# The last 64 rows of an attention tile: one full-array product and a pair of half-array products in place of two full-array products

## The chip, the cores and the metric

The kernel runs on one core of one Trainium2 chip. The metric is the time on the device in microseconds (us); the median of several executions stands for a kernel. The engines are TensorE (PE: products and transposes, with its weight loads shown as PEld), VectorE (DVE), ScalarE (ACT), GpSimd (POOL) and the queue of SyncE (SP), which issues all DMAs here.

## The reference

A linear-attention block whose output is gated by a feed-forward block, on 2048 tokens of width 576 in float32:

```python
xn = layernorm(x)                                   # 2048 x 576
q, k, v = split(xn @ wqkv)                          # 32 heads of 18
phi = lambda t: where(t > 0, t + 1, exp(t)) + 1e-6
kv = einsum("bhsd,bhse->bhde", phi(k), v)           # state of a head
num = einsum("bhqd,bhde->bhqe", phi(q), kv)
den = einsum("bhqd,bhd->bhq", phi(q), sum_s(phi(k))) + 1e-6
s = (num / den) @ wo
g = silu(gelu(xn @ w1 + b1) @ w2 + b2)              # width 4608 in between
out = x + s * g
```

## The kernel before

**Split operands.** TensorE works on a rounded float32 type. So an operand `a` is kept as a high part `h` (a ScalarE cast) and a low part `l = a - h` (a VectorE subtraction), and a product of `a` and `w` is the sum `h*wh + l*wh + h*wl`. The part `l*wl` is small and is left out nearly everywhere.

**Attention tiles.** Once the sums over all tokens are known, the state of the heads and `wo` are folded into one matrix `kw` of 576 x 576 (`fold_wo`). What is left for a tile of 128 tokens is: divide `phi(q)` by its denominators, transpose it, and multiply it by `kw`. Depth 576 is four blocks of 128 rows and a rest of 64 (rows 512 to 575). `pad` copies columns 512 to 575 of the tile once more behind its end, and the fifth block of `kw` holds its 64 rows twice, so that block 4 has 128 rows as well: rows 0 to 63 and rows 64 to 127 hold the same values.

There are 16 such tiles. Ten of them (`TO`) are done one after the other in the stage that I call the early one, lines 1327 to 1629: `transpose_p(j)` makes the five transposes into a PSUM tile `ptp`, casts all five blocks to `th` on ScalarE, and subtracts on VectorE: into `tl` for blocks 0 to 3, and for block 4 into `th` itself, rows 64 to 127 only. Block 4 of `th` is then high above and low below. `attend_mm` issues the products: per block and pair of parts two of them, for output columns 0 to 287 and 288 to 575, each into a bank of its own of the PSUM tile `ps_s`. Blocks 0 to 3 need three pairs of parts. Block 4 needs two: [h; l] by [wh; wh] and [h; l] by [wl; wl]. So a tile has (3 x 4 + 2) x 2 = 28 products. `attend(j)` casts the sums out and stores them; the first tiles are begun early by `attend_hi`, with eight of the 14 pairs of products.

The other six tiles (`LATER_TILES`) run one by one in the second half of the feed-forward stage, as class `Attention`; its methods are spread over that stage's steps by the table `A_AT`. Here `tha` and `tla` are the operands, `pta` the transposes and `psa` the sums, and `attend_mm` is the same. The weight parts lie in `Attention.kw`; `split_folded(k)` makes them once from the stored `kw`.

**The weight's block 4.** In the early stage the fold leaves block 4 in two PSUM tiles `ps_kw`; line 1209 casts them to the high part, and `last_kw_lo` subtracts the low part into `kw_l`, two subtractions of 288 columns.

**Order.** Nothing is reordered: every engine runs its instructions as the program issues them (`in_order`), and waits where an operand or a buffer is not ready. PSUM tiles of two banks (`bank2`: `ptp`, `ps_s`, `pta`, `psa`, and those of the feed-forward stage) take turns on three places; who takes a place waits for the last reader of what was there. In the early stage tile 7's sums follow `ptp7`, `ps_s6` and `ptp8`, and so take the place of `ptp7`.

Of the kernel before, what the change touches and what calls it, by code (L numbers as in the profile page):

```python
# [8 lines left out]
F32 = mybir.dt.float32  # L9
F32R = mybir.dt.float32r  # L10
# [5 lines left out]
P = 128  # L16
S = 2048
D = 576
HD = 288
# [5 lines left out]
KT = 5  # L25
# [22 lines left out]
def linear_attention_gated_ffn(ctx, tc, x, xT, wqkv, wo, w1, w1e, b1, w2, b2, out):  # L48
    nc = tc.nc
    SUB, MUL, ADD = ALU.subtract, ALU.mult, ALU.add  # L50
# [1173 lines left out]
    def last_kw_lo():  # L1224
        for _, hs, ps in last_kw:
            h, l = (w[4][:, hs] for w in kw_ops)
            nc.vector.tensor_tensor(l, ps, h.bitcast(F32), op=SUB)

    def last_kw_copy():
        for dst, _, ps in last_kw:  # L1230
# [76 lines left out]
    def transpose_only(j):  # L1307
        pb = p_bufs[j % len(p_bufs)]
        ptps[j] = pt = bank2(f"ptp{j}").rearrange("p a b -> p (a b)")
        for k in range(KT):  # L1310
            nc.tensor.transpose(pt[:, k * P : (k + 1) * P], pb[:, k * P : (k + 1) * P], ident)
# [16 lines left out]
    thp = ph2.enter_context(tc.tile_pool(name="thp", bufs=3, side="right", reuse_waits="tile"))  # L1328
    pT = {}

    def transpose_p(j):
        if j not in ptps:
            transpose_only(j)
        pt = ptps.pop(j)
        th = thp.tile([P, KT, P], F32R, tag="th", name=f"th{j}")
        tl = thp.tile([P, KT - 1, P], F32R, tag="tl", name=f"tl{j}")
        p3 = pt[:, : KT * P].rearrange("p (k c) -> p k c", k=KT)
        nc.scalar.copy(th, p3)
        nc.vector.tensor_tensor(tl, p3[:, :4, :], th[:, :4, :].bitcast(F32), op=SUB)
        nc.vector.tensor_tensor(th[64:, 4, :], p3[64:, 4, :], th[64:, 4, :].bitcast(F32), op=SUB)  # L1340
        pT[j] = (th, tl)

    transpose_p(0)
    kw_lo(1, dve)
    kw_hi(2), kw_hi(3)
    transpose_p(1)
    phi_q_hi(TO[4])
    kw_lo(2, dve), kw_lo(3, pool)
    store_kw(3)
    last_kw_lo()  # L1350
    phi_q_max(TO[4])
    pad(2)
# [7 lines left out]
    w1p = ctx.enter_context(tc.tile_pool(name="w1p", bufs=2, reuse_waits="tile"))  # L1360
    w2rp = ctx.enter_context(tc.tile_pool(name="w2rp", bufs=1, reuse_waits="tile"))
    def attend_mm(ps, th, tl, w, part=slice(None)):
        seq = [(st, v, k) for st, v in ((th, 0), (tl, 0), (th, 1)) for k in range(4)]
        seq += [(th, 0, 4), (th, 1, 4)]
        for i, (st, v, k) in list(enumerate(seq))[part]:
            for h in range(2):
                nc.tensor.matmul(  # L1367
                    ps[:, h, :HD], st[:, k, :], w[v][k][:, h * HD : (h + 1) * HD],
                    start=(i == 0), stop=(i == len(seq) - 1),
                )  # L1370

# [2 lines left out]
    def attend_hi(j):  # L1374
        ps = begun[j] = bank2(f"ps_s{j}")
        attend_mm(ps, *pT[j], kw_ops, slice(0, 8))

    def attend(j):
        ps = begun.pop(j) if j in begun else None
        if ps is None:  # L1380
            ps = bank2(f"ps_s{j}")
            attend_mm(ps, *pT.pop(j), kw_ops)
        else:
            attend_mm(ps, *pT.pop(j), kw_ops, slice(8, None))
        s_sb = stage(D, f"s{j}")
        nc.scalar.copy(as2(s_sb), ps[:, :, :HD])
        nc.sync.dma_start(s_dram[TO[j]], s_sb)
# [201 lines left out]
    attend_hi(0), attend_hi(1)  # L1589
    by_sums(4)  # L1590
    transpose_p(2)
    denominators(3), p_mult(3)
    last_kw_copy()
# [431 lines left out]
    att = None  # L2025
# [7 lines left out]
    class Attention:  # L2033
# [15 lines left out]
        def split_folded(self, k):  # L2049
            h, l = (w[k] for w in Attention.kw)  # L2050
            src = l.bitcast(F32)
            nc.scalar.copy(h, src)
            nc.vector.tensor_tensor(l, src, h.bitcast(F32), op=SUB)

        def load_sums(self):
# [47 lines left out]

        def operands(self):
            th = att.tile([P, KT, P], F32R, tag="e", name=f"tha{self.t}")
            tl = att.tile([P, KT - 1, P], F32R, tag="tl", name=f"tla{self.t}")
            p3 = self.pt[:, : KT * P].rearrange("p (k c) -> p k c", k=KT)
            nc.scalar.copy(th, p3)
            nc.vector.tensor_tensor(tl, p3[:, :4, :], th[:, :4, :].bitcast(F32), op=SUB)
            nc.vector.tensor_tensor(  # L2110
                th[64:, 4, :], p3[64:, 4, :], th[64:, 4, :].bitcast(F32), op=SUB
            )
            self.ops = th, tl

        def product(self):
            attend_mm(self.ps, *self.ops, Attention.kw)
# [36 lines left out]
    seq = ExitStack()  # L2153
    seq.enter_context(in_order(nc.vector.engine, nc.scalar.engine, nc.gpsimd.engine, nc.tensor.engine))
    n_chunks = 2 * NC
    for step in range(n_chunks):
# [3 lines left out]
        h = HOps(c)  # L2160
# [12 lines left out]
        if half == 0:  # L2173
# [7 lines left out]
            if (c, 5) not in w2_dram:  # L2181
                w = w2t[step]
# [17 lines left out]
        elif not plain:  # L2200
# [8 lines left out]
            else:  # L2209
                make(W2, w2t, step + 1)  # L2210

                w = w2t[step + 1]
# [118 lines left out]
```

## Time and profile before

| | |
|---|---|
| median of 3 runs | 1082.27 us (1081.86 to 1082.9) |
| profiled execution | 1081.32 us, span 1079.6 us |
| TensorE busy | 1071.5 us of the span, granted clock 0.999 |
| VectorE, ScalarE, GpSimd busy | 825.2, 528.3, 533.5 us |
| products of the attention tiles (L1367) | 448, each 128 x 128 weights by 288 columns |

The span runs from the first to the last instruction in the profile; the execution's time has 1.7 us around it. A row of the timeline gives the start in us from the span's start, the length of the merged record, engine, line, operation, output and inputs, active rows and columns of the array for TensorE, shapes, and a count. In brackets stands how long the engine idled before it and what ended that. The records of TensorE's products overlap, since the next starts while earlier ones are still in the array; the distance between starts is what a product costs in a stream. A row of the view of one line or tile gives minimum, median and maximum duration in ns, first and last start, and the shapes; a row of the view by groups gives the count, busy us and mean ns of one.

### The profile page before, as it was taken

Reading aid. Unit: us, or ns where it says so; the run is one execution under the profiler, and the core shown is the slowest. Engines: PE = TensorE matmul, PEld = TensorE weight load, DVE = VectorE, ACT = ScalarE, POOL = GpSimd, SP = SyncE. Lnnn points to the kernel's source line nnn. Section 1 sums busy time; section 2 is a strip of 40 time slices with the busy share of each in tenths; the row PEclk is TensorE's granted clock in tenths of the full one; section 3 lists DMA queues with packets and bytes.
Section 4 is the critical chain, followed back from the end, with each engine's and each line's share of the span. In section 5 each row is a group of like instructions: output and inputs, shape, how many; then the busy total and the mean of one; then the engine's idle time right before and its main releaser. Section 6 shows DMA issues by size and latency. Waiting matters only on the chain.

```text
span 1079.6 us, 17941 instructions
## 1 busy us (share of the span) xinstructions
PE 1071.5 (99%) x6500; PEld 990.7 (92%) x6500; DVE 825.2 (76%) x1202; ACT 528.3 (49%) x880; POOL 533.5 (49%) x552
## 2 busy tenths in 40 slices
PE   9999999999999999999999999999999999999998
PEld 7999999998998989989899898998989899998988
DVE  7997765768998898988989886485847566574856
ACT  7656657736455454554545545253443434242442
POOL 3133131658577695775957744143443525242340
PEclk9999999999999999999999999999999999999999
DMA  6678635798658577585675797796756657666653
GB/s 241 197 287 232 230 115 183 272 385 313 246 216 312 187 261 267 209 313 182 250 286 205 275 393 277 271 311 209 232 195 226 219 182 245 202 225 229 213 154 135
DMA packets 91122, 258.63 MB, mean 240 GB/s; under 512 B 12183, under 2 KB 25495, under 8 KB 88730
## 3 DMA queue, kind: packets, MB, share of 16 engines
q1 hardware_dynamic: 91034, 257.49, 68.3%
q8 instruction: 51, 0.84, 0.3%
q14 instruction: 37, 0.30, 0.1%
HBM read 155.45 MB, written 101.10 MB: 238 GB/s over the span
## 4 chain that ended last, share of the span: by engine, by line
PE 95%; DVE 2%; POOL 1%; issue 1%; DMA 1%; ACT 0%; SPq 0%; POOLq 0%; DVEq 0%
PE pm L1837 35%; PE a L1671 11%; PE zy L1671 11%; PE e L1671 11%; PE b L1671 5%; PE xaall L392 4%; PE x L392 4%; PE pd L1958 2%; PE x1all L392 2%; PE psa L1367 2%; PE ps_kva L482 1%; PE xakv L392 1%; PE x0all L392 1%; PE ps_s L1367 1%; PE x1kv L392 1%; POOL bs L1158 1%
## 5 line engine op out<-in xcount | busy, mean ns | idle before, releaser
L1774 POOL TENSOR_TENSOR g<-g 128x256 f32<-128x256 f32 x204 | 185.6, 938 | 56.9 <-DVE h_l L1419 49.9
L1843 DVE TENSOR_TENSOR macc<-pm,macc 128x576 f32<-128x576 f32 x218 | 163.8, 751 | 42.2 <-PE pm L1837 41.4
L1416 ACT CAST h_h<-g 128x512 fp32r<-128x512 f32 x204 | 122.7, 621 | 117.4 <-PE pm L1837 116.3
L1419 DVE TENSOR_TENSOR h_l<-g,h_h 128x512 fp32r<-128x512 f32 x204 | 165.1, 816 | 2.0 <-ACT h_h L1416 2.0
L1671 PE MATMUL a<-X,wa 128*128 128x512 f32 x432 | 110.2, 390 | 0.0
L1671 PEld LDWEIGHTS a<-X,wa 128*128 128x128 f32 x432 | 79.8, 188 | 15.4
L1688 ACT COPY mid<-a 128x512 f32<-128x512 f32 x36 | 21.1, 585 | 112.0 <-PE a L1671 112.0
L1774 POOL TENSOR_TENSOR mid<-g 128x256 f32<-128x256 f32 x68 | 52.0, 785 | 43.6 <-ACT g L1679 42.5
L1691 DVE TENSOR_TENSOR mid<-b,mid 128x512 f32<-128x512 f32 x36 | 24.8, 689 | 62.0 <-PE b L1671 62.0
L1467 POOL TENSOR_TENSOR w1raw<-w1raw 128x256 f32<-128x256 f32 x18 | 13.3, 739 | 91.3 <-ACT h_h L1416 47.7
L1679 ACT ACTIVATE g<-b,b1c 128x512 f32<-128x512 f32 x36 | 24.8, 689 | 66.9 <-DVE b L1697 66.8
L1671 PE MATMUL e<-X,wc 128*128 128x512 f32 x216 | 55.4, 392 | 0.0
L1671 PE MATMUL zy<-X,wd 128*128 128x512 f32 x216 | 54.9, 389 | 0.0
L1671 PE MATMUL zy<-X,wc 128*128 128x512 f32 x216 | 54.8, 389 | 0.0
L1671 PE MATMUL e<-X,wd 128*128 128x512 f32 x216 | 54.8, 389 | 0.0
L276 POOL TENSOR_TENSOR R<-R,bc 128x640 f32<-128x640 f32 x9 | 16.3, 1826 | 70.2 <-DMA R<-xT 38.8
L1671 PEld LDWEIGHTS zy<-X,wd 128*128 128x128 f32 x216 | 40.5, 188 | 8.6
L1671 PEld LDWEIGHTS e<-X,wd 128*128 128x128 f32 x216 | 40.5, 188 | 8.4
L1671 PEld LDWEIGHTS zy<-X,wc 128*128 128x128 f32 x216 | 40.5, 188 | 8.4
L1671 PEld LDWEIGHTS e<-X,wc 128*128 128x128 f32 x216 | 40.1, 188 | 8.1
L1679 ACT ACTIVATE g<-e,b1c 128x512 f32<-128x512 f32 x36 | 24.8, 689 | 45.3 <-DVE e L1704 45.3
L2090 POOL TENSOR_TENSOR qa<-qa,dena 128x576 f32<-128x576 f32 x6 | 7.0, 1168 | 62.4 <-issue 56.6
(1032 smaller groups left out, 3216.0 us busy)
## 6 DMA issues: line engine op xcount, KB each, us to landing
we<-we_dram SPq DMA_DIRECT2D x72, 224.0 KB, 5.5
w2raw<-w SPq DMA_DIRECT2D x10, 1152.0 KB
x_dram<-X SPq DMA_DIRECT2D x6, 1792.0 KB, 10.7
w1raw<-w SPq DMA_DIRECT2D x18, 512.0 KB, 4.5
op_a<-wa SPq DMA_DIRECT2D x18, 512.0 KB, 4.6
op_c<-wc SPq DMA_DIRECT2D x18, 512.0 KB, 2.6
op_d<-wd SPq DMA_DIRECT2D x18, 512.0 KB, 5.2
wc<-op_c SPq DMA_DIRECT2D x18, 512.0 KB, 5.4
```

The lines of the kernel that those rows point to most:

```text
L392: nc.tensor.matmul(dst, st, w, start=start, stop=stop, skip_group_check=True)
L1367: nc.tensor.matmul(ps[:, h, :HD], st[:, k, :], w[v][k][:, h * HD : (h + 1) * HD], start=(i == 0), stop=(i == len(seq) - 1),)
L1416: nc.scalar.copy(pair[0], src)
L1419: eng.tensor_tensor(pair[1], src, pair[0].bitcast(F32), op=SUB)
L1671: nc.tensor.matmul(ps, st, mv, start=first and n == 0, stop=n == len(seq) - 1, skip_group_check=True,)
L1679: nc.scalar.activation(g, ps, AF.Gelu_apprx_tanh, bias=b1c[:, f : f + 1])
L1688: nc.scalar.copy(m1_sb, A)
L1691: tt(u1_sb, B, m1_sb, op=ADD)
L1774: nc.gpsimd.tensor_tensor(dst[:, cs], a[:, cs], b[:, cs], op=op)
L1837: nc.tensor.matmul(ps[:, q, :HD], hs[p][st][:, cs], m[:, p, :], start=(n == 0 and i not in CHAIN), stop=(n == 5), skip_group_check=True,)
L1843: nc.vector.tensor_tensor(dst, src, dst, op=ADD)
L1958: nc.tensor.matmul(ps, st[:, cs], w_all.rearrange("p n d -> p (n d)")[:, w], start=(i == 0), stop=(i == len(seq) - 1),)
```

## The change

Block 4 is formed otherwise. The weight's second operand becomes a stack: rows 0 to 63 hold the high part once more, rows 64 to 127 the low part. The tile's high part stays as it is in all 128 rows, and its low part goes to a place of its own (`t4`, and a fifth block of `tla`). Then one pair of products over all 128 rows, `th` block 4 by [wh; wl], gives `h*wh + h*wl`. The part `l*wh` comes from two products of 64 rows: output columns 0 to 287 from rows 0 to 63 in the array's upper half, columns 288 to 575 from rows 64 to 127 in its lower half. What falls away is `l*wl` of these 64 rows. There are still 28 products in a tile.

```diff
     def last_kw_lo():
         for _, hs, ps in last_kw:
             h, l = (w[4][:, hs] for w in kw_ops)
-            nc.vector.tensor_tensor(l, ps, h.bitcast(F32), op=SUB)
+            nc.scalar.copy(l[:64], ps[:64])
+            nc.vector.tensor_tensor(l[64:], ps[64:], h[64:].bitcast(F32), op=SUB)
...
         tl = thp.tile([P, KT - 1, P], F32R, tag="tl", name=f"tl{j}")
+        t4 = thp.tile([P, P], F32R, tag="t4", bufs=2, name=f"t4{j}")
...
         nc.vector.tensor_tensor(tl, p3[:, :4, :], th[:, :4, :].bitcast(F32), op=SUB)
-        nc.vector.tensor_tensor(th[64:, 4, :], p3[64:, 4, :], th[64:, 4, :].bitcast(F32), op=SUB)
-        pT[j] = (th, tl)
+        nc.vector.tensor_tensor(t4, p3[:, 4, :], th[:, 4, :].bitcast(F32), op=SUB)
+        pT[j] = (th, [tl[:, k, :] for k in range(4)] + [t4])
...
     def attend_mm(ps, th, tl, w, part=slice(None)):
+        th = [th[:, k, :] for k in range(KT)]
         seq = [(st, v, k) for st, v in ((th, 0), (tl, 0), (th, 1)) for k in range(4)]
-        seq += [(th, 0, 4), (th, 1, 4)]
+        seq += [(th, 1, 4), (tl, 0, 4)]
         for i, (st, v, k) in list(enumerate(seq))[part]:
             for h in range(2):
+                rows = slice(64 * h, 64 * h + 64) if i == len(seq) - 1 else slice(0, P)
                 nc.tensor.matmul(
-                    ps[:, h, :HD], st[:, k, :], w[v][k][:, h * HD : (h + 1) * HD],
+                    ps[:, h, :HD], st[k][rows], w[v][k][rows, h * HD : (h + 1) * HD],
                     start=(i == 0), stop=(i == len(seq) - 1),
                 )
...
             nc.scalar.copy(h, src)
+            if k == KT - 1:
+                nc.scalar.copy(l[:64], src[:64])
+                h, l, src = h[64:], l[64:], src[64:]
             nc.vector.tensor_tensor(l, src, h.bitcast(F32), op=SUB)
...
-            tl = att.tile([P, KT - 1, P], F32R, tag="tl", name=f"tla{self.t}")
+            tl = att.tile([P, KT, P], F32R, tag="tl", name=f"tla{self.t}")
             p3 = self.pt[:, : KT * P].rearrange("p (k c) -> p k c", k=KT)
             nc.scalar.copy(th, p3)
-            nc.vector.tensor_tensor(tl, p3[:, :4, :], th[:, :4, :].bitcast(F32), op=SUB)
-            nc.vector.tensor_tensor(
-                th[64:, 4, :], p3[64:, 4, :], th[64:, 4, :].bitcast(F32), op=SUB
-            )
-            self.ops = th, tl
+            nc.vector.tensor_tensor(tl, p3, th.bitcast(F32), op=SUB)
+            self.ops = th, [tl[:, k, :] for k in range(KT)]
```

TensorE's order at the end of tile 3 of the early stage, before (`kw_l` and `kw_h` are the weight's parts, `th` the tile's high part):

```order
L1367 MATMUL ps_s_2420<-kw_l_2063,th_2362 128x288 x6
L1367 MATMUL ps_s_2420<-kw_l_2064,th_2362 128x288 x2
L1367 MATMUL ps_s_2420<-kw_h_2062,th_2362 128x288 x2
L1367 MATMUL ps_s_2420<-kw_l_2064,th_2362 128x288 x2
L1311 MATMUL ptp_2452<-ident,pbuf 128x128 x5
```

And with the change, where `t` is the new tile `t4`:

```order
L1371 MATMUL ps_s_2427<-kw_h_2062,tl_2368 128x288 x2
L1371 MATMUL ps_s_2427<-kw_l_2063,th_2367 128x288 x6
L1371 MATMUL ps_s_2427<-kw_l_2064,th_2367 128x288 x4
L1371 MATMUL ps_s_2427<-kw_h_2062,t_2369 128x288 x2
L1312 MATMUL ptp_2459<-ident,pbuf 128x128 x5
```

The two products of block 4 by the high weight's 128 rows are gone, those by the second operand have moved up, and the pair of 64 rows (the shape printed is that of the output) now ends the tile, ahead of the next transposes.

ScalarE's order where the weight's block 4 is finished, with the change; before, the row on `eq` is followed by `pbuf` at once:

```order
L434 ACTIVATE eq_2193<-eq_2193,tiny 128x576
L1227 CAST kw_l_2064<-ps_kw_2140 64x288
L1227 CAST kw_l_2064<-ps_kw_2145 64x288
L1180 COPY pbuf<-pbuf 128x64
L1340 CAST th_2266<-ptp_2260 128x640
L1232 COPY kw_1996<-ps_kw_2140 128x288
```

Two casts of 64 rows now stand ahead of the pad of tile 2 (`pbuf`), which the fifth transpose of that tile reads.

## The prediction

> **What bounds the kernel now.** I read the page's totals first, then the chain that ended last.
>
> ```profile
> span 1079.6 us, 17941 instructions
> PE 1071.5 (99%) x6500; PEld 990.7 (92%) x6500; DVE 825.2 (76%) x1202; ACT 528.3 (49%) x880; POOL 533.5 (49%) x552
> PE 95%; DVE 2%; POOL 1%; issue 1%; DMA 1%; ACT 0%; SPq 0%; POOLq 0%; DVEq 0%
> ```
>
> TensorE is busy for 99% of the span and is 95% of the chain. So a nanosecond more or less on TensorE counts fully, except where TensorE waits anyway. Next I read the products of line 1367, with their shapes kept apart, and one tile in order of time.
>
> ```profile
> L1367 PE MATMUL psa<-kw,tha x120: 290/294/302, 743.9 to 993.0; 128*128 128x288 f32 x120
> ...
> L1367 PE MATMUL ps_s<-kw_h,th x100: 288/295/401, 197.7 to 240.4; 128*128 128x288 f32 x100
> ...
> L1367 PE MATMUL ps_s<-kw_l,th x100: 292/295/377, 202.8 to 240.7; 128*128 128x288 f32 x100
> ...
> L1367 PE MATMUL ps_s<-kw_h,tl x80: 292/294/302, 199.2 to 239.1; 128*128 128x288 f32 x80
> ...
> L1367 PE MATMUL psa<-kw,tla x48: 292/294/302, 745.0 to 991.4; 128*128 128x288 f32 x48
> ```
>
> ```profile
> 743.95 1.22 PE L1367 MATMUL psa<-kw,tha 128*128 128x288 f32 x8
> 745.00 1.23 PE L1367 MATMUL psa<-kw,tla 128*128 128x288 f32 x8
> 746.07 1.75 PE L1367 MATMUL psa<-kw,tha 128*128 128x288 f32 x12
> 747.66 1.54 PE L1671 MATMUL a<-X,wa 128*128 128x512 f32 x6
> ```
>
> The rows hold 448 products: 28 in each of 16 tiles, ten between 197 and 241 us and six from 744 us on. The tile's 28 starts fill 743.95 to 747.66, so they are 0.133 us apart. Each record is 0.295 us long, so two earlier products are still in the array when one starts. That is what a switch of the array's layout could have to wait for: 0.295 - 0.133 = 0.162 us.
>
> Where does TensorE wait in these stretches? Only the early one has waits that can swallow something.
>
> ```profile
> 222.91 0.42 PE L1367 MATMUL ps_s<-kw_l,th 128*128 128x288 f32 x2
> 223.48 0.77 PE L1311 MATMUL ptp<-ident,vb 128*128 128x128 f32 x5
> ...
> 227.80 0.71 PE L1311 MATMUL ptp<-ident,pbuf 128*128 128x128 f32 x5
> 229.03 1.29 PE L1367 MATMUL ps_s<-kw_h,th 128*128 128x288 f32 x8 [0.53 <-DVE th L1340]
> ```
>
> ```profile
> L1311 PE MATMUL ptp<-ident,vb 128*128 128x128 f32 x30 | 4.3, 274 | 0.1
> ```
>
> ```profile
> 227.89 0.69 DVE L1339 TENSOR_TENSOR tl<-ptp,th 128x512 fp32r<-128x512 f32 x1
> 228.59 0.29 DVE L1340 TENSOR_TENSOR th<-ptp,th 64x128 fp32r<-64x128 f32 x1
> ```
>
> Five transposes span 0.71 us and one record is 0.274 long, so their starts are (0.71 - 0.274) / 4 = 0.109 us apart. So tile 7 could have started at 227.80 + 5 x 0.109 = 228.35 and started at 229.03: 0.69 us of waiting. At 223.48 it is 0.30 us (222.91 + 2 x 0.133 = 223.18). Together 1.0 us by which tiles 0 to 6 can be later at no cost, and which swallows what they gain. Is the wait at 229.03 removed? Its releaser is the subtraction that the change takes out of `th`. But the product waits there for PSUM: three bank pairs are used in turn, and tile 7's sums take the pair of its own transposes, whose last reader is that subtraction. The new one, into `t4`, reads the same pair at the same place. The wait stays.
>
> **VectorE.** Line 1340 becomes a subtraction over 128 rows instead of 64.
>
> ```profile
> L545 DVE SCALAR_TENSOR_TENSOR wa_rest0ef<-wa_rest0gm,sgn,wa_rest0ef 64x512 f32<-64x512 f32 x1 | 0.8, 752 | 0.0
> ...
> L543 DVE SCALAR_TENSOR_TENSOR wa_rest0ef<-wa_rest0ef,sgn 128x512 f32<-128x512 f32 x1 | 0.7, 671 | 0.0
> ```
>
> Sixty-four rows are no cheaper than 128 for the same columns, so ten times 0.29 us stay 0.29, and so do the two halved ones of line 1227. In the six late tiles two subtractions become one of 640 columns. From 0.69 us for 512 columns and 0.29 for 128, a column costs 1.03 ns, and the one takes 0.82 instead of 0.98 us: 0.16 us less on VectorE, six times. It buys nothing.
>
> ```profile
> 742.41 0.69 DVE L2109 TENSOR_TENSOR tla<-pta,tha 128x512 fp32r<-128x512 f32 x1 [2.93 <-ACT tha L2108]
> 743.13 0.29 DVE L2110 TENSOR_TENSOR tha<-pta,tha 64x128 fp32r<-64x128 f32 x1
> ```
>
> It had ended at 743.42, and TensorE came to the tile in its own order at 743.95.
>
> **ScalarE.** Added are two casts of 64x288 ahead of `pad(2)`, and one of 64x576 behind the splits of the folded weight.
>
> ```profile
> 201.37 0.23 ACT L1180 COPY pbuf<-pbuf 128x64 f32<-128x64 f32 x1
> 203.11 0.69 ACT L1338 CAST th<-ptp 128x640 fp32r<-128x640 f32 x1 [1.51 <-PE ptp L1311]
> 203.70 0.71 ACT L1231 COPY kw<-ps_kw 128x288 f32<-128x288 f32 x2
> ```
>
> ```profile
> 727.58 2.39 ACT L2052 CAST kw<-kw 128x576 fp32r<-128x576 f32 x4
> 734.02 0.59 ACT L1688 COPY mid<-a 128x512 f32<-128x512 f32 x1 [4.05 <-PE a L1671]
> ```
>
> By the 0.71 us of two copies of that length, `pad(2)` ends at 202.31 instead of 201.60.
>
> ```profile
> 202.37 0.71 PE L1311 MATMUL ptp<-ident,pbuf 128*128 128x128 f32 x5
> ```
>
> Only the fifth transpose reads the pad, at 202.37 + 4 x 0.109 = 202.81. Half a microsecond is left, and behind it ScalarE idles 1.51 us. Without that cover the 0.71 us would go on TensorE once. The late cast (some 0.6 us, a quarter of 2.39) has 4.05 idle us behind it. ScalarE: nothing.
>
> **TensorE.** Each tile keeps 28 products. The last two shrink from 128 rows to 64, one in each half of the array and each into its own bank. So there are two unknowns: whether they run at once, and what going to 64 rows and back costs. No product of 64 rows stands in the trace. The nearest rows are six products that use 8 of the array's columns.
>
> ```profile
> 192.52 0.30 PE L392 MATMUL x1q<-wT1h,X 128*128 128x288 f32 x1
> 192.65 0.30 PE L1200 MATMUL ps_kw<-wT4h,wT1h 72*8 72x288 f32 x1
> ...
> 193.31 0.29 PE L1200 MATMUL ps_kw<-wT4h,wT1l 72*8 72x288 f32 x1
> 193.44 0.29 PE L392 MATMUL xaq<-wT4h,X 128*128 128x288 f32 x1
> ```
>
> Going in takes 0.13 us and coming back 0.13 us: no price. But there only the outputs narrow, and sums still run down all rows. In the new pair the sums of the two halves must leave the array apart, while the full products ahead, two of them still inside, add both. That is why I do not carry the free switch over. The lower end for a switch is 0; for the upper end the array empties first.
>
> In the upper case, counted from the start of the last full product: it leaves at 0.295, and the pair starts then, not at 0.133. The full product behind starts another 0.295 later, at 0.590, where three steps of 0.133 made 0.400. That is 0.191 us more a tile if the pair runs at once and all weights are loaded meanwhile. If the loads wait for the switch too, 0.109 comes in at each end (starts of transposes are no closer, at 128 columns to load and to stream): 0.409. If the pair runs one after the other as well, 0.133 more: 0.542. No row is nearer to either of the first two, so I take their middle, 0.300.
>
> The Trainium skill, page "TensorEngine Tiling (Array Packing)", section "Key Properties", says that a change of the tiling mode drains TensorE. By it the sum is the upper case; the trace shows no such drain for the columns (0.13 us in, 0.13 out) and nothing for the rows.
>
> Sum: 16 x 0.300 = 4.8 us, less the 1.0 us that the waits at 223 and 229 swallow: 3.8 us. The profiled execution took 1081.32 us (span 1079.6 and 1.7 around it), so 1085.1 by it; the median of the three runs, 1082.27, lies 0.95 above, so I predict **1086.1 us**. The forecast's own range goes from 16 x 0.191 - 1.0 = 2.1 us (1084.4) to 16 x 0.542 - 1.0 = 7.7 us (1090.0).
>
> **Rivals.** First: the switch is free, as for the columns, and the pair overlaps. If the two start together, a tile saves 0.133 us. If the second waits until its weights are in, its load begins with the first product and takes 0.109, and a tile saves 0.02. What tiles 0 to 6 save is lost in the wait at 229.03, so nine tiles count: 0.2 to 1.2 us, 1081.1 to 1082.1 us, middle 1081.6. For it speaks the free switch at 192.65, against it that the rows' sums must part. The Trainium skill, page "TensorE: Matmul & The Clock Gate", section "The mechanism", has products in different row groups start about 4 ns apart. By that it is the far end, 1081.1; no row here shows it.
>
> Second, the change does not do what it says: free switch, but the halves run in turn. Then 28 steps of 0.133 remain and the time stays 1082.3.
>
> Third, faster: the halves run at once and the saving of the early tiles is kept too, because the VectorE and POOL work that ends in the wait at 229.03 moves up with TensorE. That is 16 x 0.133 = 2.1 us, and with the six late tiles' 0.16 us on VectorE, if it shortens a wait, up to 3.1: 1079.2 to 1080.1. Against it: the work behind 229.03 is named VectorE, not TensorE.
>
> **How the numbers follow.** Forecast 0.50, first rival 0.32, second 0.10, third 0.08. A difference of 0.2%, 2.2 us, is about what a measurement of this kernel can tell from no change. Faster by that is the third rival: 0.08. The first two lie within: 0.42. Slower is the forecast, whose low end just reaches the bound: 0.50. The range takes in the first rival and all but the dearest of the forecast (0.542 a tile): 1081.0 to 1089.0.
>
> **What would show it.** In the changed profile: in a late tile, 26 products at 0.133 steps, then a gap of 0.16 us or more ahead of the first 64-row product and another ahead of the next full one. Two free steps of 0.13 there would sink the forecast. The starts of the two 64-row records tell whether they run at once: some ns apart, 0.11, or 0.133. The wait at 229.03 should still end with a VectorE subtraction, and the transposes near 202.4 should show no new wait on ScalarE.

## The result, and the profile after

| | before | changed |
|---|---|---|
| median of 13 runs | 1081.44 us (1080.75 to 1082.90) | 1084.43 us (1083.73 to 1086.99) |
| ratio, 95% interval | | 1.0030 [1.0022, 1.0037] |
| span of the profiled execution | 1079.6 us | 1082.2 us |
| TensorE busy | 1071.5 us | 1075.1 us |
| VectorE busy, instructions | 825.2 us, 1202 | 817.4 us, 1196 |

The change makes the kernel 3.0 us slower, 0.30%; 3.8 us had been forecast. The two profiled executions, read below, differ by 2.6 us. The totals and the chain by engine, from the page of the changed kernel:

```profile
span 1082.2 us, 17941 instructions
PE 1075.1 (99%) x6500; PEld 990.1 (91%) x6500; DVE 817.4 (76%) x1196; ACT 529.7 (49%) x883; POOL 535.0 (49%) x552
PE 97%; POOL 1%; DMA 1%; ACT 0%; issue 0%; DVE 0%; SPq 0%; ACTq 0%; DVEq 0%
```

TensorE still bounds the kernel. Its share of the chain went from 95% to 97%, and VectorE's from 2% to 0: VectorE no longer ends a wait that counts.

What a tile now costs is read in the last late tile. First the starts of TensorE's products in the changed kernel (start, length of the merged record, count at the end of the row), then the weight loads of the same place,

```profile
993.95 1.50 PE L1371 MATMUL psa<-kw,tha 128*128 128x288 f32 x10
995.37 0.40 PE L1371 MATMUL psa<-kw,tla 64*128 64x288 f32 x2
995.70 1.65 PE L1675 MATMUL a<-X,wa 128*128 128x512 f32 x6
997.19 0.39 PE L1675 MATMUL a<-RX,we 128*128 128x512 f32 x1
```

```profile
994.75 0.45 PEld L1371 LDWEIGHTS psa<-kw,tha 128*128 128x128 f32 x3
995.37 0.19 PEld L1371 LDWEIGHTS psa<-kw,tla 64*128 64x128 f32 x2 [0.17 <-issue]
995.70 0.53 PEld L1675 LDWEIGHTS a<-X,wa 128*128 128x128 f32 x3
```

and, from the view of line 1371, the durations of the 64-row products of the early stage (minimum, median, maximum in ns):

```profile
L1371 PE MATMUL ps_s<-kw_h,t x20: 392/393/397, 204.4 to 241.6; 64*128 64x288 f32 x20
```

Four things stand in these rows.

- **The pair runs at once.** Two records of about 0.393 us make one merged record of 0.40 us, so the two starts lie within some ns; the single records of the trace have them 3 to 4 ns apart.
- **Going in waits.** The tenth full product starts at 993.95 + 9 x 0.133 = 995.15, and the pair 0.22 us later, where 0.133 was the step. That is 0.09 us.
- **The weights wait too.** In a stream a load, 0.19 us long, begins with the product before its own and is mostly hidden under it. Here the loads idle for 0.17 us and start at 995.37, at the same time as the pair's products: nothing is loaded ahead across the switch. So the records of the pair are 0.39 us long instead of 0.295; by this reading some 0.10 us of each is its own weight load. The switch is not the only place of this: behind the wait at 223.48 us in the kernel before, the first transpose starts with its own load, and five of them fill 0.77 us there instead of 0.71.
- **Coming out is the same again.** The next full product starts 0.33 us after the pair: 0.10 of load, 0.133 of streaming, 0.09 of emptying. Its own load begins with it and is not hidden either: its six products take 1.49 us to the next row, where before it was 1.38 (747.66 to 749.04).

Measured are the distances between starts. That the 0.09 us is the array running empty is a reading: the pair starts 0.07 us before the record of the product ahead ends, and no row shows the array itself.

Before, the first late tile and the six products behind it ended with this start:

```profile
749.04 0.39 PE L1671 MATMUL a<-RX,we 128*128 128x512 f32 x1
```

From the tile's start at 743.95 that is 5.09 us. The first late tile of the changed kernel shows the two ends:

```profile
744.80 1.22 PE L1371 MATMUL psa<-kw,tha 128*128 128x288 f32 x8
...
748.35 0.40 PE L1371 MATMUL psa<-kw,tla 64*128 64x288 f32 x2
748.68 1.65 PE L1675 MATMUL a<-X,wa 128*128 128x512 f32 x6
750.17 0.40 PE L1675 MATMUL a<-RX,we 128*128 128x512 f32 x1
```

744.80 to 750.17 is 5.37 us: 0.28 us more, of which the step-by-step sum (two switches of 0.09 + 0.11, less one step of 0.133 that the overlap saves) explains 0.27.

In the early stage the wait that a VectorE subtraction ended is gone. TensorE comes later than VectorE is done:

```profile
228.68 0.40 PE L1371 MATMUL ps_s<-kw_h,t 64*128 64x288 f32 x2
229.01 0.76 PE L1312 MATMUL ptp<-ident,pbuf 128*128 128x128 f32 x5
229.53 1.30 PE L1371 MATMUL ps_s<-kw_h,th 128*128 128x288 f32 x8
```

```profile
228.59 0.28 DVE L1342 TENSOR_TENSOR t<-ptp,th 128x128 fp32r<-128x128 f32 x1
```

Tile 7 starts at 229.53 with no wait; its PSUM place had been read out at 228.87. That is 0.50 us later than before, and 0.11 of it is the stage's own later start (its first transposes stand at 195.41 us, before at 195.30). The seven tiles ahead had lost about 1.6 us (0.26 for each of the first two, behind which products follow, 0.21 for the five with transposes behind them). So the old waits swallowed 1.1 to 1.2 us: the 0.99 us of waiting itself and, behind each wait, a load that was not hidden. The 0.21 is read here too: five transposes take 0.52 us to the next product, 0.05 more than the 0.47 of the kernel before, where coming out costs a full product 0.11:

```profile
232.82 0.71 PE L1311 MATMUL ptp<-ident,vb 128*128 128x128 f32 x5
233.29 1.31 PE L1367 MATMUL ps_s<-kw_h,th 128*128 128x288 f32 x8
```

The first transposes of the stage and the first product of the feed-forward stage, before and after:

```profile
195.30 0.71 PE L1311 MATMUL ptp<-ident,vb 128*128 128x128 f32 x5
...
240.82 1.55 PE L1671 MATMUL a<-X,wa 128*128 128x512 f32 x6
```

```profile
195.41 0.71 PE L1312 MATMUL ptp<-ident,vb 128*128 128x128 f32 x5
...
241.92 0.96 PE L1675 MATMUL a<-X,wa 128*128 128x512 f32 x3
```

The stage grows from 45.52 to 46.51 us, by 1.0. The rest of the span, with the six late tiles in it, grows from 838.8 us (1079.6 - 240.82) to 840.3 (1082.2 - 241.92), by 1.5.

### The profile page after: what moved, and what is told of

Read it like the earlier page. It is cut to its first block, busy times and chain, and to the rows that moved or that the text cites. A ratio compares the mean times of both kernels' runs of the same rounds, so it can differ in the third digit from the quotient of the medians.

```text
span 1082.2 us, 17941 instructions
## 1 busy us (share of the span) xinstructions
PE 1075.1 (99%) x6500; PEld 990.1 (91%) x6500; DVE 817.4 (76%) x1196; ACT 529.7 (49%) x883; POOL 535.0 (49%) x552
## 4 chain that ended last, share of the span: by engine, by line
PE 97%; POOL 1%; DMA 1%; ACT 0%; issue 0%; DVE 0%; SPq 0%; ACTq 0%; DVEq 0%
PE pm L1841 35%; PE a L1675 11%; PE zy L1675 11%; PE e L1675 11%; PE b L1675 5%; PE xaall L392 4%; PE x L392 4%; PE ps_s L1371 3%; PE pd L1962 2%; PE x1all L392 2%; PE psa L1371 2%; PE ps_kva L482 1%; PE xakv L392 1%; PE x0all L392 1%; PE x1kv L392 1%; PE ptp L1312 0%
```

## The experiments

The theory after the result: **a row switch costs twice.** Each change between the full layout and the 64-row layout empties the array (0.09 us over a step) and then leaves one weight load unhidden (0.10 to 0.11 us). Two switches a tile are 0.40 us, the overlap gives 0.133 back. The rivals: the added casts and subtractions are to blame (A); 64-row products are slow in themselves (B); the pair does not really overlap (C); the early waits swallow nothing (D); the price grows with the product ahead (E). All times over before are against runs of the kernel before on the same chip, 1081.03 us in the first four experiments and 1081.41 in the other three.

### The same edits, but 96 rows

```diff
-                rows = slice(64 * h, 64 * h + 64) if i == len(seq) - 1 else slice(0, P)
+                rows = slice(0, 96) if i == len(seq) - 1 else slice(0, P)
```

> As the change, but the two last products take rows 0 to 95 instead of 64 rows each, so they stay in the array's full layout (32 of the 64 low rows by the high weight are counted twice in the output). All edits on ScalarE and VectorE stay. Theory (the price is two switches of the array's layout a tile, each emptying the array, about 0.09 us, and then loading weights unhidden, about 0.11 us): no switch, 28 steps of 0.133 us, time as before within 0.5 us, 1081.4. Rival A (the added casts and subtractions delay the tiles): 3 us slower as the change, 1084.4.

Measured: 1081.66 us, 0.6 over before by the medians and 0.3 by the ratio, 1.0003 [0.9994, 1.0012]; the interval goes from 0.6 us faster to 1.3 us slower. The end of the last late tile:

```profile
993.02 0.69 PE L1371 MATMUL psa<-kw,tha 128*128 128x288 f32 x4
993.55 0.43 PE L1371 MATMUL psa<-kw,tla 96*128 96x288 f32 x2
993.82 1.09 PE L1675 MATMUL a<-X,wa 128*128 128x512 f32 x4
```

Two products of 96 rows take 0.27 us, two steps of 0.133, and what follows comes at once. Everything else of the change is in this kernel, so the casts and subtractions cost nothing that can be measured, and rival A with its 3 us falls. The early stage also answers a point of the prediction:

```profile
228.63 0.71 PE L1312 MATMUL ptp<-ident,pbuf 128*128 128x128 f32 x5
229.66 0.63 PE L1371 MATMUL ps_s<-kw_h,th 128*128 128x288 f32 x3 [0.31 <-DVE t L1342]
```

Without the switches the wait ahead of tile 7 is there again, and it ends with the subtraction into `t4`. Taking the subtraction out of `th` did not take the wait away, since it is one for the PSUM place.

### Both products in the same half

```diff
-                rows = slice(64 * h, 64 * h + 64) if i == len(seq) - 1 else slice(0, P)
+                rows = slice(0, 64) if i == len(seq) - 1 else slice(0, P)
```

> As the change, but both 64-row products use rows 0 to 63, the same half of the array. Theory: the switches stay, the overlap goes; the second starts 0.133 us after the first instead of 0.004, 16 x 0.13 = 2.1 us over the change, 1086.5, 5.1 over before. Rival B (a product of 64 rows is slow in itself, 0.324 us, with no price for the layout): the second takes another 0.324, 5.2 us over the change, 1089.6. Rival C (the records of the overlapping pair deceive, and it runs in turn anyway): as the change, 1084.4.

Measured: 1085.82 us, 4.8 over before, ratio 1.0040 [1.0027, 1.0053].

```profile
996.94 0.56 PE L1371 MATMUL psa<-kw,tha 128*128 128x288 f32 x3
997.43 0.53 PE L1371 MATMUL psa<-kw,tla 64*128 64x288 f32 x2
997.89 1.19 PE L1675 MATMUL a<-X,wa 128*128 128x512 f32 x4
```

The next full product now comes 0.46 us after the first of the two, not 0.33: without overlap the second costs one more step of 0.13. So the overlap in the change is real (C falls by this step; the two times alone are too close), and a second 64-row product costs no second 0.32 (B falls). The step is the one that was forecast, and the 4.8 us agree with the 5.1 forecast over before (the interval goes from 2.9 to 5.7 us). The time lies 0.7 us under the stated 1086.5; 0.4 of that is the kernel before, which took 1081.03 us in these runs and 1081.44 in those that the statement started from.

The same rows also tell the load from the switch. The second of the two follows inside the layout, and yet it starts 0.23 to 0.24 us after the first (0.53 less a record of 0.295), a step and 0.10 us: the first one's unhidden load.

### The pair twice

```diff
-        seq += [(th, 1, 4), (tl, 0, 4)]
+        seq += [(th, 1, 4), (tl, 0, 4), (tl, 0, 4)]
...
-                rows = slice(64 * h, 64 * h + 64) if i == len(seq) - 1 else slice(0, P)
+                rows = slice(64 * h, 64 * h + 64) if i >= len(seq) - 2 else slice(0, P)
```

> As the change, but the pair of 64-row products is issued twice at a tile's end (the low part by the high weight is counted twice in the output). Theory: a further pair inside the 64-row layout costs one step, 0.133 us, 16 x 0.133 = 2.1 us over the change, 1086.5. Rival B (64-row products slow in themselves): 0.324 us a pair, 5.2 us over the change, 1089.6.

Measured: 1086.34 us, 5.3 over before where 5.1 was forecast, ratio 1.0048 [1.0035, 1.0060].

```profile
997.59 0.54 PE L1371 MATMUL psa<-kw,tla 64*128 64x288 f32 x4
998.05 0.97 PE L1675 MATMUL a<-X,wa 128*128 128x512 f32 x3
```

Four 64-row products, two pairs, take 0.46 us to the next full product where one pair takes 0.33. A further pair inside the layout costs 0.13 us. So the price lies at the border of the layout and not in the products.

### Two more switches

```diff
+        steps = [(i, s, h) for i, s in enumerate(seq) for h in range(2)]
+        steps.sort(key=lambda s: (min(s[0], len(seq) - 2), s[2] if s[0] > len(seq) - 3 else 0))
```

The products are issued in the order of `steps`: full, 64 rows above, full, 64 rows below.

> As the change, but the order at a tile's end is full product, 64 rows upper half, full product, 64 rows lower half: four switches a tile instead of two, and no overlap. The same 28 products. Theory: 4 x 0.20 = 0.80 us a tile over before, 16 x 0.80 = 12.8 less the 1.0 us that the waits at 223 and 229 us swallow: 11.8 over before, 1093.2. Rival B (each 64-row product 0.324 instead of 0.133, no price for switching): 0.38 a tile, 6.1 less 1.0, 5.1 over before, 1086.5.

Measured: 1091.99 us, 11.0 over before, ratio 1.0098 [1.0085, 1.0112].

```profile
1002.01 0.69 PE L1375 MATMUL psa<-kw,tha 128*128 128x288 f32 x4
1002.63 0.40 PE L1375 MATMUL psa<-kw,tla 64*128 64x288 f32 x1
1002.95 0.40 PE L1375 MATMUL psa<-kw,tha 128*128 128x288 f32 x1
1003.28 0.39 PE L1375 MATMUL psa<-kw,tla 64*128 64x288 f32 x1
1003.60 1.43 PE L1679 MATMUL a<-X,wa 128*128 128x512 f32 x5
```

Between two switches each step is 0.32 to 0.33 us, whether a full product or a 64-row one stands there: 0.19 over a step, the 0.09 of emptying and the 0.10 of loading. The full product in the middle is just as slow as its 64-row neighbours, which no theory of slow 64-row products allows. The time was expected 0.8 us higher, inside the interval (9.2 to 12.1 us over before). The trace accounts for most of it: a tile with transposes behind it takes 0.71 us more than before (two of them 9.96 us from transposes to transposes, 222.28 to 232.24, where one took 4.27, 214.64 to 218.91) and not 0.80, which is 0.5 us over six tiles, and the waits swallow 1.1 to 1.2 us instead of 1.0.

### Early tiles alone, late tiles alone

In the first kernel the late tiles, in the second the early ones, keep operands, weight parts and products as before; for this `attend_mm` stands in the kernel twice. The core of the second one's edit:

```diff
         def product(self):
-            attend_mm(self.ps, *self.ops, Attention.kw)
+            attend_mm_pair(self.ps, *self.ops, Attention.kw)
```

> The change in the ten early tiles alone; the six late ones as before. Theory: from the changed profile a tile costs 0.26 us more where products follow and 0.21 where transposes follow: 4 x 0.26 + 6 x 0.21 = 2.3 us, less 1.0 us that TensorE waited there before: 1.3 over before, 1082.7. Rival D (the early waits move along with TensorE and swallow nothing): 2.3 over, 1083.7.

> The change in the six late tiles alone; the ten early ones as before. Theory: 6 x 0.264 = 1.6 us over before, 1083.0. Rival D (the early stage pays in full, so less is left here: 3.0 - 2.3): 0.7 over, 1082.1.

Measured: early alone 1082.64 us, 1.2 over before, ratio 1.0011 [1.0003, 1.0020]; late alone 1083.58 us, 2.2 over, ratio 1.0020 [1.0011, 1.0029]. The early value is near the theory's 1.3. Its interval, 0.3 to 2.2 us, just leaves rival D's 2.3 out; the late value is above the theory's 1.6, with an interval of 1.2 to 3.1 us that holds it and leaves rival D's 0.7 out. The two add up to 3.4 us with intervals that take in the 3.0 of the whole change.

The traces separate the two better than the times, since the stretch ahead of the early stage ends at another moment in each execution. The rows that begin and end that stage, with the early tiles changed alone and with the late ones alone:

```profile
195.69 0.71 PE L1312 MATMUL ptp<-ident,vb 128*128 128x128 f32 x5
...
242.23 1.19 PE L1685 MATMUL a<-X,wa 128*128 128x512 f32 x4
```

```profile
196.62 0.71 PE L1311 MATMUL ptp<-ident,vb 128*128 128x128 f32 x5
...
242.18 1.31 PE L1683 MATMUL a<-X,wa 128*128 128x512 f32 x5
```

| | early stage | rest of the span |
|---|---|---|
| before | 45.52 us | 838.8 us |
| early tiles alone (span 1081.1 us) | 46.54 us | 838.9 us |
| late tiles alone (span 1082.5 us) | 45.56 us | 840.3 us |
| whole change | 46.51 us | 840.3 us |
| 96 rows (span 1080.3 us) | 45.31 us | 838.9 us |

The early tiles cost 1.0 us in their stage, the late ones 1.5 in the rest, and neither stretch changes by more than 0.1 us when the other's tiles are changed. The 2.3 us that rival D needs in the early stage are not there. With 96 rows (196.11 to 241.42) neither stretch is longer than before by more than 0.1, which speaks once more against rival A. Of these 2.3 us of added steps the last load, 0.1, falls behind the stage's end, so the old waits swallowed about 1.2. The 2.2 us of the late tiles alone also hold a later start of the early stage, 1.3 us in the profiled execution, and nothing ahead of that stage was changed.

### The pair first

The kernel with the change in the late tiles alone, and there:

```diff
-        seq += [(th, 1, 4), (tl, 0, 4)]
+        seq = [(tl, 0, 4), *seq, (th, 1, 4)]
...
-                rows = slice(64 * h, 64 * h + 64) if i == len(seq) - 1 else slice(0, P)
+                rows = slice(64 * h, 64 * h + 64) if i == 0 else slice(0, P)
```

> As the run with the change in the late tiles alone, but the 64-row pair comes first in a tile: behind a product of 512 columns, and ahead of one of 288. Theory: what a switch costs does not depend on the length of the product ahead, the pair starts 0.227 + 0.09 = 0.32 us after that product, 1.6 over before, as the run without the move. Rival E (the wait grows with the length of the product ahead, 0.224/0.133 times its step): 0.38 us, another 6 x 0.065 = 0.4 us, 2.0 over before.

Measured: 1082.92 us, 1.5 over before, ratio 1.0014 [1.0005, 1.0023].

```profile
990.06 0.61 PE L1683 MATMUL zy<-X,wd 128*128 128x512 f32 x2
990.51 0.39 PE L1683 MATMUL zy<-RX,we 128*128 128x512 f32 x1
990.83 0.40 PE L1379 MATMUL psa<-kw,tla 64*128 64x288 f32 x2
991.15 0.80 PE L1379 MATMUL psa<-kw,tha 128*128 128x288 f32 x4
```

Behind a product of 512 columns the pair starts after 0.32 us, 0.09 over that product's step (two of them fill 990.06 to 990.51, 0.225 each). For these two lengths the price is a constant, not a share of the product ahead, so rival E falls in the trace; the times alone, 2.0 against 1.6, could not have told. Nor do they tell a difference between the pair first and the pair last (1.5 us, 0.5 to 2.5, against 2.2, 1.2 to 3.1).

No version that beats the kernel before came out of this. A stay in the 64-row layout costs 2 x (0.09 + 0.11) = 0.40 us and each overlapping pair in it saves 0.133, so by this estimate three pairs would only break even, and a tile has one. No kernel with more pairs in a stay that are of use to the result was built.

## Why the prediction was right

**The sign and the mechanism** were right: TensorE sets the time, and the switch into the 64-row layout and back costs more than the overlap saves. The run with 96 rows and the one with two more switches show it, one with none and the other with twice as many. The stated time was 1086.1 us and 1084.4 was measured: 0.8 of the difference is the starting value, 1082.27 from three runs where thirteen gave 1081.44, and 0.8 is the change itself.

**The term of the sum, 0.300 us a tile,** was near for a mixed reason. I had set the emptying of the array at 0.162 us, the whole of what a record is longer than a step; it is 0.09. I had left open whether the weight loads wait for the switch and taken the middle; they do wait, at both ends. That the middle came near is luck: an emptying taken too long and a load counted by half offset each other. By the measured sizes the prediction's case of waiting loads, 0.409, becomes 0.409 - 2 x 0.07 = 0.27, and 0.28 was seen in a late tile. Ahead of transposes it is less, about 0.21, and the prediction had one price for all tiles. Transposes are 0.109 apart anyway, and that step looks like the price of their loads, since nine products of 192 columns, half as many again as a transpose has, stand no further apart ((1.14 - 0.27) / 8 = 0.109):

```profile
1073.45 1.14 PE L1958 MATMUL pd<-w_plain,hp 128*128 128x192 f32 x9
```

So 10 x 0.23 + 6 x 0.27, less the 1.2 that the waits swallowed, is 2.7 us; the profiled executions differ by 2.6, the medians by 3.0.

**The swallowed 1.0 us** was right in kind and a little small: the early tiles add some 2.3 us of steps, the stage grows by 1.0, and 1.1 to 1.2 were swallowed. The sum had counted the waits up to the next start and not the unhidden load behind it. The prediction's check that the wait ahead of tile 7 would still end with a VectorE subtraction did not hold in the changed kernel, because that wait was swallowed whole, as the prediction's own seven tiles at 0.300 us against 1.0 us of waiting would have it; with 96 rows it is there, released by the subtraction into `t4`.

**VectorE and ScalarE at nothing** was right. The one subtraction of 640 columns takes 0.825 us, where 0.82 was worked out, and two casts end in time for the pad:

```profile
L2116 DVE TENSOR_TENSOR tla<-pta,tha x6: 825/825/825, 743.3 to 989.5; 128x640 fp32r<-128x640 f32 x6
```

```profile
201.48 0.67 ACT L1227 CAST kw_l<-ps_kw 64x288 fp32r<-64x288 f32 x2
202.04 0.25 ACT L1180 COPY pbuf<-pbuf 128x64 f32<-128x64 f32 x1
203.23 0.70 ACT L1340 CAST th<-ptp 128x640 fp32r<-128x640 f32 x1 [0.94 <-PE ptp L1312]
```

The pad ends at 202.29 (202.31 was worked out), and ScalarE still idles 0.94 us behind it.

**The first rival** was half right: the pair overlaps at once, with starts 4 ns apart, its far end. Its other half, that going to 64 rows is as free as going to 8 columns at 192.65 us, is what failed. The second (halves in turn) fell with the run that kept both in one half. The third, faster, had no saving to keep: each tile cost 0.2 to 0.3 us more.

The Trainium skill, page "TensorEngine Tiling (Array Packing)", section "Key Properties", has a change of the tiling mode drain TensorE. For rows the trace fits that: 0.09 us, and the weight load behind it. The products on 8 columns follow at 0.13 us in both kernels, with no drain; whether 8 columns make another tiling mode, no record here shows, so they do not speak against the page.

## What to carry to other kernels

Before splitting a product into halves of the array, count the borders, not the products: here one stay in the 64-row layout cost 0.40 us on a stream of 0.133 us products, and a pair that overlaps gives back one step, so up to three pairs in one stay win nothing. By these runs a product of 96 or of 72 rows costs nothing extra: those of 96 rows stood 0.13 us apart with what follows at once, and those of 72 rows ahead of the first transposes start 0.13 us apart too, from 194.77 us on in the kernel before. And where an engine bounds a kernel, look in each stage for the waits it still has: here they took in half of what the ten early tiles had to pay, 1.2 of 2.3 us.

## What the runs showed of the hardware

I had not expected going to 64 rows and going to 8 columns to differ as they do. Six products that use 72 rows and 8 of the 128 columns stand at steps of 0.13 us between full ones, in and out, in the kernel before. A switch to 64 rows costs about 0.20 us each way, and what it adds to the next start does not depend on whether the product ahead has 288 columns (0.22 against a step of 0.133) or 512 (0.32 against 0.225). Nor had I expected a start in the records to stand ahead of its own weight load: behind a switch the product and its load begin together, and the load shows up as 0.10 us more in the product's record, and as a late start of the product after it. A wait does the same: at 223.48 us in the kernel before, a transpose and its load begin together too.
